# Attention and two mixer blocks on one core: four more pairs of heads take their scores from unsplit fp32 q and k

## Chip, cores and metric

The kernel runs on one core of a Trainium2 chip. The metric is the device time of one execution in microseconds, and lower is better. Three runs of the kernel before took 925.19, 927.50 and 928.23 us; their median, 927.5 us, is the time before.

## What is computed

The reference is a causal attention over 4 batches, 12 heads, 448 positions and a head dimension of 64, followed by two mixer blocks on the joined heads:

```python
scores = scale * np.matmul(q, k.transpose(0, 1, 3, 2))
scores = np.where(mask, -1000000000.0, scores)
scores = scores - np.max(scores, axis=-1, keepdims=True)
attn = np.exp(scores)
attn = attn / (np.sum(attn, axis=-1, keepdims=True) + 1e-09)
attn_out = np.matmul(attn, v)
...
h = np.maximum(xt @ w_tok1, 0.0) @ w_tok2
u = x + h.transpose(0, 2, 1)
h2 = np.maximum(u @ w_ch1, 0.0) @ w_ch2
x = u + h2
...
theta = x @ w_theta
y = w_tok_r @ (x * cos(theta)) + w_tok_i @ (x * sin(theta))
u = x + y
out = u + np.maximum(u @ w_ch, 0.0)
```

All inputs are fp32 or wider (the weights are 64-bit floats), and the kernel keeps close to fp32 accuracy throughout.

## The kernel before

Attention works on pairs of heads: 4 batches of 6 pairs, so 24 pairs, numbered from 0. Pairs 6 to 11 are the second batch. Each pair has seven tiles of scores (the list `TILES`): one of 128 query rows by 128 keys that holds the first 64 positions of both heads, and two each (one per head) with 192, 320 and 448 keys.

There are two ways to make the scores, and the set `NATIVE` (line 30) says which pairs take which. A pair in the set has **native** scores: q and k are loaded into 64 partitions, the other 64 are set to zero by POOL (line 215), and one plain fp32 matmul makes a tile (line 274, `ps_sc<-k_pad,q_raw`). Every other pair has **split** scores: q and k are loaded twice over into 128 partitions, and each is split by ACT and DVE into a high part of the matmul's rounded fp32 type and the rest (`qs`, `kh`, `kl`, lines 231 to 236); two matmuls in that type, with kh and with kl, make a tile (lines 274 and 276), and a tile of 128 or 192 keys is computed with 256 columns. Before, pairs 0 to 7 are native. The lines that matter:

```python
        if b * NPR + pr in NATIVE:
            kr = ap2.tile([P, 2 * S], F32, tag="kh", name="k_pad")
            for t, src in ((kr, k), (qr, q)):
                (nc.vector if b * NPR + pr == 0 else nc.gpsimd).memset(t[64:128], 0.0)
...
            copy_to(pick("qhi"), qs, qr)
            rest_to(pick("qlo"), qs[64:128], qr[64:128], qs[64:128])
            copy_to(pick("khi"), kh, kr)
            rest_to(pick("klo"), kl, kr, kh)
...
        nc.tensor.matmul(ps[:, 0:n], lhsT=lhs, rhs=cut(pp.kh), start=True, stop=pp.kl is None)
        if pp.kl is not None:
            nc.tensor.matmul(ps[:, 0:n], lhsT=lhs, rhs=cut(pp.kl), start=False, stop=True)
```

Buffers: the raw q and k of all pairs share the tag `qk_raw`, which has two buffers. A native pair holds one of them with its q from the load to its last score matmul (its k lies in the tag `kh`, two buffers too). A split pair holds one with q and one with k, and each only until ACT and DVE have split it.

After the scores DVE masks a tile and finds its maximum (line 281, from one of three banks `ps_sc`), ACT takes the exponentials (line 283), and the tile is transposed for the product with v. Pairs 0 to 11 (the set `NATPV`, not changed) have it transposed by PE (line 290) and multiplied in fp32 (line 318). Pairs 12 to 23 have it split into two 16-bit parts `ph` by ACT (line 111) and DVE (line 303), in one of three buffers, transposed by a DMA from SP's queue (`pt<-ph`, line 306) and multiplied in many small matmuls (line 329). Two pairs together give `xg` (line 345, ACT) for a token mixer (lines 354 to 372), whose results fill the four banks `ps_mm` along with everything else on PE; line 367 is the ACT copy that empties one of them.

Beside attention run 72 channel-mixer "units" of 18 matmuls each (`mm3`, lines 170 to 172, 448 columns), placed by the table `UNIT_STEPS`, and the rounding of the 64-bit weights: a raw tile is fetched (line 124, `raw<-in_w_ch_dram`), ACT and DVE round and split it (lines 127 to 138, 118), and it is stored. After attention, from about 530 us, the second mixer runs, which the change does not touch.

The order of the instructions on each engine is set when the program is built: a scheduler with a timeline of its own picks, from what is ready by that timeline, what stands next in each queue, with attention at high priority. Every engine then works through its queue in that order, and a wait at the head holds up all that is behind it. So a change in one place gives other orders from there on.

Of the kernel before, what the change touches and what calls it, by code (L numbers as in the profile page):

```python
# [26 lines left out]
NEG = -1.0e30  # L27
PSC = 32768.0
BUFS = dict(ut=9, h2=6, acc=12, ws=4, wf=2, raw=2, sb=3, ph=3, pt=5)
NATIVE = {0, 1, 2, 3, 4, 5, 6, 7}  # L30
NATPV = {0, 1, 2, 3, 4, 5, 6, 7, 8, 9, 10, 11}
AHEAD, LAG, LOOK = 500, 4, 2
KEEP, UBACK = 6, 16
# [20 lines left out]
def fused(ctx, tc, q, k, v, w_tok1, w_tok2, w_ch1, w_ch2, w_theta, w_tok, w_ch, out):  # L54
# [155 lines left out]
    def prep(b, pr):  # L210
        qr = ap2.tile([P, 2 * S], F32, tag="qk_raw", name="q_raw", bufs=2)
        if b * NPR + pr in NATIVE:
            kr = ap2.tile([P, 2 * S], F32, tag="kh", name="k_pad")
# [12 lines left out]
        nc.sync.dma_start(out=vr, in_=v[b, pr])  # L226
        if b * NPR + pr in NATIVE:
            qs, kh, kl = qr, kr, None
# [558 lines left out]
```

## Time and profile before

| what | value |
|---|---|
| time, median of 3 runs | 927.5 us |
| time of the profiled execution | 925.87 us |
| span of its instructions, first to last | 924.1 us |
| PE busy with matmuls, loading weights | 900.6 us (97%), 825.6 us (89%) |
| DVE, ACT, POOL busy | 633.5 us (69%), 388.2 us (42%), 109.9 us (12%) |
| native scores, first and last start | 4.7 and 108.0 us |
| split scores, first and last start | 113.2 and 462.3 us |
| idle of ACT before line 111's `ph`, for `pt<-ph` | 66.5 us |
| loads of a split pair's q, its k: size, median to landing | 448 KB, 5.3 us; 448 KB, 6.3 us |
| loads of a native pair's k, its q | 224 KB, 3.8 us; 224 KB, 4.1 us |

Times are counted from the span's start. The 1.8 us between the span and the profiled execution's own time lie outside of the first and last instruction. A matmul's time in the trace runs to its modelled end and overlaps the next one's: what a matmul costs PE is the distance from its start to the next start, if nothing waits. PE's share of busy time is therefore not its share of useful time, but idle time before a matmul is real. `PE` rows are matmuls, `PEld` rows their weight loads, `SPq` rows the issues of SP's queue.

### The profile page before, as it was taken

Reading aid. Unit: us, or ns where it says so; the run is one execution under the profiler, and the core shown is the slowest. Engines: PE = TensorE matmul, PEld = TensorE weight load, DVE = VectorE, ACT = ScalarE, POOL = GpSimd, SP = SyncE. Lnnn points to the kernel's source line nnn. Section 1 sums busy time; section 2 is a strip of 40 time slices with the busy share of each in tenths; the row PEclk is TensorE's granted clock in tenths of the full one; section 3 lists DMA queues with packets and bytes.
Section 4 is the critical chain, followed back from the end, with each engine's and each line's share of the span. In section 5 each row is a group of like instructions: output and inputs, shape, how many; then the busy total and the mean of one; then the engine's idle time right before and its main releaser. Section 6 shows DMA issues by size and latency. Waiting matters only on the chain.

```text
span 924.1 us, 15928 instructions
## 1 busy us (share of the span) xinstructions
PE 900.6 (97%) x5820; PEld 825.6 (89%) x5820; DVE 633.5 (69%) x1468; ACT 388.2 (42%) x914; POOL 109.9 (12%) x177
## 2 busy tenths in 40 slices
PE   7999999997999999999999999999999999999998
PEld 5988999896898898989899999999999999999997
DVE  6799797998987777467774288845864566575341
ACT  6788677675655555344532144321211212202100
POOL 2110000000000000000000000021631233242120
PEclk9999999998999999999999999999999999999999
DMA  6677994789999979699797899864505225054033
GB/s 184 190 254 254 360 335 172 251 300 272 260 316 317 285 207 263 223 275 290 199 322 244 280 326 369 281 195 132 184 1 162 78 86 179 19 162 128 6 133 129
DMA packets 104687, 199.17 MB, mean 216 GB/s; under 512 B 60896, under 2 KB 72992, under 8 KB 104608
## 3 DMA queue, kind: packets, MB, share of 16 engines
q1 hardware_dynamic: 103296, 196.35, 67.9%
q0 software_dynamic: 1152, 1.57, 0.9%
q8 instruction: 46, 0.75, 0.3%
q14 instruction: 33, 0.27, 0.1%
q10 hardware_dynamic: 160, 0.23, 0.1%
HBM read 149.36 MB, written 34.60 MB: 199 GB/s over the span
## 4 chain that ended last, share of the span: by engine, by line
PE 81%; DMA 10%; DVE 6%; issue 1%; ACT 1%; SPq 1%; ACTq 0%; DVEq 0%
PE ps_mm L170 18%; PE ps_mm L172 18%; PE ps_mm L171 18%; DMA pt<-ph 6%; PE ps_sc L274 3%; PE ps_sc L172 3%; PE ps_sc L170 3%; PE ps_sc L171 3%; PE ps_pv L318 3%; PE ps_pv L329 3%; DMA raw<-in_w_ch_dram 2%; PE ps_mm L290 2%; PE ps_sc L276 1%; PE ps_mm L355 1%; PE ps_mm L356 1%
## 5 line engine op out<-in xcount | busy, mean ns | idle before, releaser
L170 PE MATMUL ps_mm<-h,ws 128*128 128x448 f32 x432 | 159.4, 370 | 2.1 <-DMA ws<-w_c 1.3
L171 PE MATMUL ps_mm<-h,ws 128*128 128x448 f32 x432 | 159.2, 369 | 0.0
L172 PE MATMUL ps_mm<-h,ws 128*128 128x448 f32 x432 | 158.6, 368 | 0.0
L172 PE MATMUL ps_mm<-ut,ws 128*128 128x448 f32 x288 | 106.4, 369 | 0.0
L170 PE MATMUL ps_mm<-ut,ws 128*128 128x448 f32 x288 | 106.3, 369 | 0.0
L171 PE MATMUL ps_mm<-ut,ws 128*128 128x448 f32 x288 | 105.9, 368 | 0.0
L283 ACT ACTIVATE sb<-sb,mx 128x192 f32<-128x192 f32 (+3 forms) x168 | 89.3, 532 | 32.4 <-DVE mx L281 31.4
L170 PEld LDWEIGHTS ps_mm<-h,ws 128*128 128x128 f32 x432 | 81.2, 188 | 9.7 <-DMA ws<-w_c 1.6
L172 PEld LDWEIGHTS ps_mm<-h,ws 128*128 128x128 f32 x432 | 81.2, 188 | 7.0
L171 PEld LDWEIGHTS ps_mm<-h,ws 128*128 128x128 f32 x432 | 81.2, 188 | 6.8
L281 DVE CUSTOM_DVE_ANT_0 sb<-ps_sc,mask 128x192 f32<-128x192 f32 (+3 forms) x168 | 74.2, 455 | 10.2 <-PE ps_mm L290 5.8
L114 POOL TENSOR_SCALAR ut<-acc 128x448 fp32r<-128x448 f32 x24 | 17.4, 731 | 474.9 <-PE ps_mm L171 454.3
L591 ACT ACTIVATE tmp<-ps_sc 128x384 f32<-128x384 f32 x28 | 13.5, 482 | 132.3 <-PE ps_sc L172 132.1
L303 DVE SCALAR_TENSOR_TENSOR ph<-sb,ph 128x64 f16<-128x64 f32 (+3 forms) x156 | 42.8, 318 | 33.2 <-ACT ph L111 32.4
L318 PE MATMUL ps_pv<-v_raw,ptf 128*128 128x128 f32 (+1 forms) x456 | 63.6, 275 | 1.4 <-issue 0.9
L318 PEld LDWEIGHTS ps_pv<-v_raw,ptf 128*128 128x128 f32 x456 | 59.6, 192 | 5.7 <-issue 2.3
L111 ACT ACTIVATE ph<-sb 128x192 f16<-128x192 f32 (+3 forms) x84 | 36.5, 443 | 66.9 <-DMA pt<-ph 66.5
L172 PEld LDWEIGHTS ps_mm<-ut,ws 128*128 128x128 f32 x288 | 54.2, 188 | 4.5 <-issue 0.2
L170 PEld LDWEIGHTS ps_mm<-ut,ws 128*128 128x128 f32 x288 | 54.2, 188 | 4.5 <-issue 0.2
L171 PEld LDWEIGHTS ps_mm<-ut,ws 128*128 128x128 f32 x288 | 54.2, 188 | 4.2
L388 DVE SCALAR_TENSOR_TENSOR h<-ps_mm,h 128x448 fp32r<-128x448 f32 x48 | 29.7, 619 | 31.3 <-ACT h L387 31.2
L598 ACT ACTIVATE tmp<-tmp 128x384 f32<-128x384 f32 x28 | 14.7, 526 | 86.0 <-DVE tmp L596 86.0
(152 smaller groups left out, 2113.7 us busy)
## 6 DMA issues: line engine op xcount, KB each, us to landing
ws<-w_c SPq DMA_DIRECT2D x107, 768.0 KB, 5.5
raw<-in_w_ch_dram SPq DMA_DIRECT2D x30, 768.0 KB, 6.3
w_c<-ws SPq DMA_DIRECT2D x30, 768.0 KB, 6.6
q_raw<-in_q_dram SPq DMA_DIRECT2D x16, 448.0 KB, 5.3
k_raw<-in_k_dram SPq DMA_DIRECT2D x16, 448.0 KB, 6.3
v_raw<-in_v_dram SPq DMA_DIRECT2D x24, 288.0 KB, 4.9
x2d<-acc SPq DMA_DIRECT2D x24, 224.0 KB, 4.8
acc<-x2d SPq DMA_DIRECT2D x24, 224.0 KB, 3.6
```

Of the source, the lines that this page charges most:

```text
L111: nc.scalar.activation(dst, src, AF.Copy, scale=scale)
L170: nc.tensor.matmul(ps, lhsT=ka(a[:, 0]), rhs=kb(b[:, 0]), start=first, stop=False)
L171: nc.tensor.matmul(ps, lhsT=ka(a[:, 0]), rhs=kb(b[:, 1]), start=False, stop=False)
L172: return nc.tensor.matmul(ps, lhsT=ka(a[:, 1]), rhs=kb(b[:, 0]), start=False, stop=last)
L274: nc.tensor.matmul(ps[:, 0:n], lhsT=lhs, rhs=cut(pp.kh), start=True, stop=pp.kl is None)
L281: pp.first = nc.vector.tensor_tensor_reduce(out=dst, in0=src, in1=msk, op0=ALU.add, op1=ALU.min, scale=-0.125, scalar=3.0e38, accum_out=pp ...
L283: pp.last = nc.scalar.activation(sb[:, 0:kk], sb[:, 0:kk], AF.Exp, bias=pp.mx[:, j:j + 1], scale=-1.0, accum_out=pp.sm[:, j:j + 1])
L290: nc.tensor.transpose(pst[:, u * P:(u + 1) * P], full[:, c0 + u * P:c0 + (u + 1) * P], ident)
L303: nc.vector.scalar_tensor_tensor(out=dst, in0=sb[:, c0:c1], scalar=PSC, in1=hi[:, c0:c1], op0=ALU.mult, op1=ALU.subtract)
L318: pp.pv = nc.tensor.matmul(pp.ps[:, reg:reg + n], lhsT=pt[:, u], rhs=pp.v[0][:, vt * D:vt * D + n], start=(u == 0), stop=(u == len(blks) - 1))
L329: pp.pv = nc.tensor.matmul(pp.ps[:, reg:reg + D], lhsT=pt[:, blk], rhs=pp.v[c][:, vt * D:(vt + 1) * D], start=(n == 0), stop=(n == len(job ...
L388: gates[0] = nc.vector.scalar_tensor_tensor(out=t[:, 1], in0=ps[:, 0:S], scalar=0.0, in1=f32v(t[:, 0]), op0=ALU.max, op1=ALU.subtract)
```

## The change

Pairs 8 to 11 join the set. Nothing else in the source differs:

```diff
-NATIVE = {0, 1, 2, 3, 4, 5, 6, 7}
+NATIVE = {0, 1, 2, 3, 4, 5, 6, 7, 8, 9, 10, 11}
```

By instructions: PE has 28 split score matmuls at line 274 and 28 at line 276 fewer for 28 native ones more (8 tiles of 448, 8 of 320, 8 of 192 and 4 of 128 keys). ACT has 8 copies of 128x896 fewer, DVE 4 of `kl` and 4 of `qs` fewer, POOL 8 memsets of 64x896 more. SP's queue has 8 loads of 128x896 fewer for 8 of 64x896 more.

The built orders differ in many places from pair 8 on. Three of them follow. The first is **SP's queue** from the loads of pair 11 or 12 to those of pair 14. The `L222` and `L224` rows are loads of a split pair's q and k. Before, pairs 12, 13 and 14 are `q_raw_2189`, `q_raw_2378` and `q_raw_2670`:

```order
L222 DMA q_raw_2189<-in_q_dram 128x896
L124 DMA raw_1811<-in_w_ch2_dram 128x1536
L224 DMA k_raw_2191<-in_k_dram 128x896
L448 DMA w_c2_0_2_107<-ws_1807 128x1536
L124 DMA raw_1895<-in_w_ch2_dram 128x1536
L226 DMA v_raw_1916<-in_v_dram 128x576
L124 DMA raw_1966<-in_w_ch2_dram 128x1536
L448 DMA w_c2_0_3_108<-ws_1891 128x1536
L448 DMA w_c2_1_4_115<-ws_1962 128x1536
L222 DMA q_raw_2378<-in_q_dram 128x896
L224 DMA k_raw_2380<-in_k_dram 128x896
```

and in the change pairs 12 and 13 are `q_raw_2147` and `q_raw_2330`:

```order
L448 DMA w_c2_1_4_115<-ws_1926 128x1536
L222 DMA q_raw_2147<-in_q_dram 128x896
L124 DMA raw_1954<-in_w_ch1_dram 128x1536
L448 DMA w_c2_0_4_109<-ws_1950 128x1536
L224 DMA k_raw_2149<-in_k_dram 128x896
L124 DMA raw_2098<-in_w_ch1_dram 128x1536
L448 DMA w_c2_0_5_110<-ws_2094 128x1536
L222 DMA q_raw_2330<-in_q_dram 128x896
L224 DMA k_raw_2332<-in_k_dram 128x896
```

Before, q of pair 12 stood ahead of the stores `w_c2_0_2` to `w_c2_1_4`; in the change it stands behind them. In the built program of the change pair 11's q lies in one buffer of `qk_raw`, and q of 12, k of 12, q of 13 and k of 13 all have the address of the other, which q of pair 10 held before them. Before, the q and k of pair 12 have two addresses, and so have those of 13.

The second place is **ACT** in the change, while pair 11 (`sb`, `sm_2136`) begins. `kh_2156` is pair 12's, `qs_2336` pair 13's; `ps_mm_2016` to `ps_mm_2061` are banks that the token mixer fills:

```order
L357 ACTIVATE h1_2015<-ps_mm_2016 128x256
L111 ACTIVATE kh_2156<-k_raw_2149 128x896
L357 ACTIVATE h1_2015<-ps_mm_2031 128x256
L367 ACTIVATE acc_2051<-ps_mm_2046 128x448
L111 ACTIVATE qs_2336<-q_raw_2330 128x896
L367 ACTIVATE acc_2066<-ps_mm_2061 128x448
```

The copy that empties `ps_mm_2061` stands behind the split of pair 13's q. The next unit on PE, `ps_mm_2115`, has that bank's address.

The third place is **PE** where pair 12's product with v begins. Before, between the last matmul of the first three tiles and the first of the next tile (`pt_2469`):

```order
L329 MATMUL ps_pv_2495<-v_mid_2202,pt_2444 128x64
L274 MATMUL ps_sc_2723<-kh_2387,qs_2384 128x256
L276 MATMUL ps_sc_2723<-kl_2389,qs_2384 128x256
L354 MATMUL ps_mm_2502<-xg0_2282,wt1_146 128x256
L354 MATMUL ps_mm_2517<-xg0_2282,wt1_146 128x256
L363 MATMUL ps_mm_2532<-ident2_128,x0_154 128x64
L365 MATMUL ps_mm_2532<-ident_123,x0_154 128x128 x3
L274 MATMUL ps_sc_2757<-kh_2387,qs_2384 128x256
L276 MATMUL ps_sc_2757<-kl_2389,qs_2384 128x256
L329 LDWEIGHTS pt_2469
```

and in the change the same place begins as follows:

```order
L329 MATMUL ps_pv_2447<-v_mid_2160,pt_2396 128x64
L354 MATMUL ps_mm_2454<-xg0_2237,wt1_146 128x256
L354 MATMUL ps_mm_2469<-xg0_2237,wt1_146 128x256
L363 MATMUL ps_mm_2484<-ident2_128,x0_154 128x64
L365 MATMUL ps_mm_2484<-ident_123,x0_154 128x128 x3
L355 MATMUL ps_mm_2454<-xg1_2238,wt1_146 128x256
L356 MATMUL ps_mm_2454<-xg0_2237,wt1_146 128x256
L354 MATMUL ps_mm_2454<-xg0_2237,wt1_146 128x256
```

There the whole token mixer (24 matmuls of 256 columns), 8 transposes by PE, 6 score matmuls and 6 matmuls of the mixer's second half stand ahead of the next tile's first line-329 matmul.

## Rows read from the trace of the kernel before

**Rows 1.** Windows: us; PE, PEld, DVE, ACT, POOL busy (x count); PEclk, DMA share, GB/s

```profile
150.00:175.00 25.00, 25.00 (x171) 23.80 (x170) 22.41 (x48) 17.79 (x40) 0.00 (x0) 1.00 0.70 242
175.00:200.00 25.00, 23.96 (x160) 21.87 (x159) 23.32 (x50) 16.55 (x38) 0.00 (x0) 1.00 0.74 258
200.00:225.00 25.00, 18.76 (x139) 17.12 (x138) 21.02 (x58) 16.38 (x40) 0.00 (x0) 0.86 1.07 290
225.00:250.00 25.00, 22.91 (x198) 20.55 (x196) 23.02 (x58) 15.22 (x38) 0.00 (x0) 1.00 1.00 267
```

**Rows 2.** Waits from 175 to 250 us: us in total, times, longest

```profile
PE ps_pv L329 <- DMA pt<-ph: 5.7, 3, 3.0
...
PE ps_mm L170 <- ACT acc L367: 0.8, 1, 0.8
```

**Rows 3.** Timeline of PE, 211 to 220 us: start, us, instruction [idle before <-releaser]

```profile
211.42 0.20 PE L329 MATMUL ps_pv<-v_raw,pt 128*128 128x64 bf16 x1 [0.62 <-DMA pt<-ph]
...
215.27 0.50 PE L354 MATMUL ps_mm<-xg,wt 128*128 128x256 f32 x2 [2.60 <-ACT xg L111]
...
219.72 0.23 PE L329 MATMUL ps_pv<-v_raw,pt 128*128 128x64 bf16 x1 [3.02 <-DMA pt<-ph]
```

**Rows 4.** Windows, the stretch behind those waits

```profile
220.00:224.00 4.00, 4.00 (x30) 4.00 (x28) 3.31 (x12) 2.72 (x7) 0.00 (x0) 0.55 1.04 359
```

**Rows 5.** Timeline of PE: native scores, each with the instruction behind it

```profile
28.52 0.70 PE L274 MATMUL ps_sc<-k_pad,q_raw 128*128 128x320 f32 x2
29.06 0.49 PE L290 MATMUL ps_mm<-ident,sb 128*128 128x128 f32 x3
29.38 0.92 PE L274 MATMUL ps_sc<-k_pad,q_raw 128*128 128x448 f32 x2
30.14 0.50 PE L318 MATMUL ps_pv<-v_raw,ptf 128*128 128x128 f32 x3
...
78.67 0.49 PE L274 MATMUL ps_sc<-k_pad,q_raw 128*128 128x192 f32 x2
79.00 0.60 PE L290 MATMUL ps_mm<-ident,sb 128*128 128x128 f32 x4
```

**Rows 6.** Timeline of PE: split scores, first matmul and the instruction behind the second

```profile
169.22 0.28 PE L274 MATMUL ps_sc<-kh,qs 128*128 128x256 f32 x1
...
169.46 0.36 PE L170 MATMUL ps_mm<-h,ws 128*128 128x448 f32 x1
...
202.41 0.32 PE L274 MATMUL ps_sc<-kh,qs 128*128 128x320 f32 x1
...
202.71 0.31 PE L274 MATMUL ps_sc<-kh,qs 128*128 128x320 f32 x1
...
207.74 0.37 PE L274 MATMUL ps_sc<-kh,qs 128*128 128x448 f32 x1
...
208.15 0.36 PE L171 MATMUL ps_mm<-ut,ws 128*128 128x448 f32 x1
```

**Rows 7.** Tile q_raw: count, ns min/median/max, first to last start; its loads' landing

```profile
L111 ACT ACTIVATE qs<-q_raw x16: 934/937/952, 96.1 to 416.6; 128x896 fp32r<-128x896 f32 x16
L118 DVE TENSOR_TENSOR qs<-q_raw,qs x16: 1087/1089/1091, 97.1 to 418.0; 64x896 fp32r<-64x896 f32 x16
...
DMA to landing us min/median/max: 2.1/4.6/10.5
```

**Rows 8.** Tile k_raw, the same columns

```profile
L111 ACT ACTIVATE kh<-k_raw x16: 934/940/958, 104.8 to 415.6; 128x896 fp32r<-128x896 f32 x16
L118 DVE TENSOR_TENSOR kl<-k_raw,kh x16: 1071/1086/1093, 106.5 to 416.6; 128x896 fp32r<-128x896 f32 x16
...
DMA to landing us min/median/max: 4.2/6.3/7.5
```

**Rows 9.** Timeline: pair 12's first tile, its score on PE and its maximum on DVE

```profile
194.62 0.37 PE L274 MATMUL ps_sc<-kh,qs 128*128 128x256 f32 x1
...
199.60 0.28 DVE L281 CUSTOM_DVE_ANT_0 sb<-ps_sc,mask 128x128 f32<-128x128 f32 x1
```

## The prediction, made before the change was run

> **What bounds the kernel now.** I read the windows first. Pairs 8 to 11 were scored between 113 and 198 us. From 150 to 175 us PE is busy for all of its 25.00 us, and no wait of PE shows there; DVE is busy for 22.41 us of them [rows 1]. So in this stretch the program moves as fast as PE's queue, and DVE, though close, is not what ends last. From 175 us that changes: PE loses 25.00 - 23.96 = 1.0 us, then 6.2, then 2.1 us, 9.4 in all [rows 1]. The list of waits says for what: 5.7 us for three landings of DMA transposes of pairs 12 and 13, the first pairs that are transposed so, and 0.8 for ACT emptying a bank [rows 2]. The timeline puts most of it in one place, the start of pair 12's product with v: 0.62 us before its first matmul, 2.60 before the token mixer, which waits for ACT's xg, and 3.02 before the next tile's product [rows 3]. After these pauses the granted clock reads 0.55 from 220 to 224 us, with PE busy throughout [rows 4]: some 90% of that stretch at the lower of its two levels, 1.2 of 2.4 GHz, which costs about half of 3.6 us, 1.8 us. A reader should see two things: work added to PE before 175 us costs its full time, and between 200 and 224 us lie 6.2 us of waits and 1.8 us of slow clock that a different order could win back.
>
> **PE's own work.** What a tile costs is the distance between starts [rows 5, 6]. 448 keys: native 30.14 - 29.38 = 0.76 us, split 208.15 - 207.74 = 0.41, so +0.35. 320 keys: 29.06 - 28.52 = 0.54 against 202.71 - 202.41 = 0.30, +0.24. 192 keys: 79.00 - 78.67 = 0.33 against 169.46 - 169.22 = 0.24 (the split form computes 256 columns), +0.09. 128 keys: two thirds of 0.33 is 0.22, an estimate, against 0.24, -0.02. A pair has two of each of the first three and one of the last: 2 x 0.68 - 0.02 = 1.34. Four pairs: **+5.4 us**. No gap of PE hides it: it falls before and beside 113 to 198 us, where the waits are 1.0 us in all.
>
> The Trainium skill has a rule that speaks against the change: by "FP8 and Floating Point Precision", TensorE Precision Notes, true fp32 takes four passes through the array. With a split matmul as one pass (0.205, 0.15 and 0.12 us here), four passes would make 0.82, 0.60, 0.35 and 0.23 us, a pair +1.63 and the term +6.5 us; the rows give a little less than four passes, and the sum goes by the rows.
>
> **What ACT, DVE and POOL lose and gain.** A split costs ACT 0.937 + 0.940 us and DVE 1.089 + 1.086 us [rows 7, 8]; four pairs make 7.5 us on ACT and 8.7 us on DVE. Where PE is full this is worth nothing by itself: DVE only comes closer to being on time. The 8 memsets fall on POOL, which does nothing at all from 150 to 250 us [rows 1], and a pair's loads have the time of a whole pair, some 20 us. I count both as nothing; without that cover a late memset would hold SP's queue, and through it the weight loads. The smaller loads (64 partitions for 128) I count as nothing too: no PE wait before 175 us is one for a load.
>
> **The hand-over from pair 11 to pair 12.** Here the change makes a chain. q of 12, k of 12, q of 13 and k of 13 go through one buffer, each after the split of the one before, and the first only after pair 10's last score matmul, because pair 11's native q holds the other buffer. Counted from there: q of 12 lands after 4.6 (the median), ACT and DVE split it in 0.94 + 1.09 [rows 7], 6.6 us; k of 12 takes 6.3 + 0.94 + 1.09 [rows 8], 14.9 us; q of 13 takes 4.6 + 0.94 on ACT, 20.4 us. Behind that copy stands ACT's line 367, about half a microsecond (I take 0.5), which empties the bank that the next unit needs: 20.9 us. Between the same score and that unit PE's queue holds 50 matmuls of 448 columns at 0.205 (half of the 0.41 above, 10.2 us), 24 of the token mixer at 0.12 (2.9), four native tiles of 128, 192, 192 and 320 keys (1.4), and 37 small fp32 matmuls and transposes, some of them twice as long (about 5.4 in all): 19.9 us. So at median landings PE waits **1.0 us**, about what it loses there already [rows 1]: net 0. That is the most uncertain term. If everything lands at the least (2.1, 4.2, 2.1) it is 0 and the present 1.0 us is gone; one q that takes 10.5 us adds 5.9. DVE stands still during these landings, so pair 12 begins with DVE late, and it is late already: the first tile's score stands at 194.62 and DVE takes it up at 199.60, 5.0 us later [rows 9]. PE's cover between that score and the first line-329 matmul grows by only 1.2 us (17.2 for 16.0). I take **+0.7 us** more at the first wait, between 0 and +3.
>
> **Pair 12's product.** In the profile the next tile's product starts 219.72 - 211.42 = 8.3 us after the first [rows 3]; that is the way through ACT, DVE and one more transpose, because there are only three buffers `ph`. PE had 1.8 us of work in it, 0.6 for the first three tiles and 1.2 behind them. In the new order the whole token mixer and more stands there: 24 x 0.12 + 8 transposes at 0.11 + 6 score matmuls (0.84) + 6 x 0.205 = 5.9 us, with the first tiles 6.5. Of the waits 8.3 - 6.5 = 1.8 us remains for 2.60 + 3.02 = 5.6: **-3.8 us**. With pauses so much shorter I count half of the slow clock as gone, **-0.9**. Bounds: 0 if ACT and DVE are later by as much, -7.4 if both go fully. The native pairs show some short waits of their own in the first 100 us; I put **+0.6** on pairs 8 to 11, between 0 and 2.
>
> Sum: 5.4 + 0.0 + 0.7 - 3.8 - 0.9 + 0.6 = **+2.0 us**. The profiled execution took 925.87 us, with a span of 924.1, so the changed one should take about 927.9. It lies 1.6 below the median of the three runs; on 927.5 the forecast is **929.5 us**.
>
> **The rivals.** First, slower: the landings decide. PE's work covers 19.9 us of a chain of 20.9, so from there on each microsecond of a late landing is one of the end time. For it: q's landing reaches 10.5 us [rows 7], and in the new order weight tiles stand between these loads on the same queue. Against it: the DMA share from 150 to 200 us is 0.70 to 0.74, not the 1.07 of later [rows 1]. With one load at its maximum 929.5 + 5.9 = 935.4 us.
>
> Second, faster: DVE is what makes the waits, and 8.7 us less of it let pair 12 start on time, so that all waits of 175 to 224 us go. For it: the 5.0 us by which DVE is late at pair 12 [rows 9]. Against it: the splits of 12 and 13 stay, and the splits that go are those before. Then 5.4 - (1.0 + 0.6 + 5.6 + 1.8) = -3.6: 923.9 us.
>
> Third, no change: the forecast holds, and the remaining transposes' wait at pair 13, 5.7 - 0.62 - 3.02 = 2.1 us [rows 2, 3], goes as well, since pair 12 is spread over more work: 927.4 us.
>
> That the change does not do what it says can be left out: the counts of instructions show 28 native matmuls for 56.
>
> **How the numbers follow.** A measurement here can tell 0.3% from no change, 2.8 us: 924.7 to 930.3. The forecast, about 928 to 932, has a chance of 0.45, of which 0.31 lie within 0.3% and 0.14 above. The late landings, 932 to 938, have 0.26, all above. The faster case has 0.16, of which 0.01 lies within. The third has 0.13, all within. So faster 0.15, within 0.3% 0.45, slower 0.40. The forecast's own range is 928 to 932. For 8 in 10 the range takes in the faster case's point and the late landings up to one load at its maximum with a microsecond and a half on top: 923.8 to 937.
>
> **What would show it.** Right: 28 more native score matmuls at 0.76, 0.54 and 0.33 us from start to start; PE without idle time up to about pair 11; a wait of some 1 us for ACT line 367 there; less than 3 us of PE's waits for xg and `pt<-ph` at pair 12, and a granted clock of 1 behind it. Wrong: a wait of several microseconds for ACT or DVE behind a q or k load before pair 12 (the first rival), no waits from 175 to 224 us (the second), or waits at pair 12 as long as before.

## The result and the profile after

The changed kernel took 933.59 us (median of 6 runs, 932.36 to 937.58), the kernel before beside it 926.40 (6 runs). The ratio is 1.0091, 95% interval 1.0072 to 1.0111: slower by 0.9%. Measured once more, beside another set of runs of before, it was 1.0058 (1.0035 to 1.0080), so the change costs some 5 to 8 us where 2 were forecast. The profiled execution of the change took 933.34 us, its span is 931.6: 7.5 us more than the span of before.

The page's part 1, first line (busy us, share, instructions), of the change:

```profile
PE 906.6 (97%) x5820; PEld 826.7 (89%) x5820; DVE 627.0 (67%) x1460; ACT 381.7 (41%) x906; POOL 115.9 (12%) x185
```

PE is busy for 6.0 us longer (900.6 before) and idle for 1.5 us longer (25.0 for 23.5). DVE and ACT were each busy for 6.5 us less (the splits that went make 8.6 and 7.5 us, instruction by instruction), and the kernel is slower all the same. The windows of the change, with the columns of [rows 1]:

```profile
150.00:175.00 25.00, 25.00 (x156) 22.23 (x156) 22.33 (x49) 15.21 (x36) 1.64 (x2) 1.00 0.80 260
175.00:200.00 25.00, 23.11 (x146) 20.96 (x144) 19.56 (x43) 14.80 (x34) 0.00 (x0) 1.00 0.61 207
200.00:225.00 25.00, 22.11 (x166) 20.52 (x165) 24.23 (x62) 17.89 (x40) 0.00 (x0) 1.00 0.93 285
225.00:250.00 25.00, 22.23 (x168) 19.32 (x167) 18.89 (x49) 15.64 (x40) 0.00 (x0) 1.00 1.02 268
...
250.00:475.00 225.00, 221.98 (x1856) 201.88 (x1855) 161.86 (x441) 113.33 (x279) 0.00 (x0) 0.99 0.94 264
475.00:931.60 456.60, 450.05 (x2407) 416.90 (x2403) 264.44 (x522) 100.01 (x211) 94.47 (x150) 1.00 0.52 169
```

From 175 to 250 us PE is idle for 1.89 + 2.89 + 2.77 = 7.6 us where it was 9.4 [rows 1], and in this execution the clock no longer falls there. Behind 250 us it is the other way round. For the kernel before the two last windows read:

```profile
250.00:475.00 225.00, 222.78 (x1833) 202.34 (x1832) 161.63 (x440) 114.37 (x281) 0.00 (x0) 1.00 0.95 267
475.00:924.10 449.10, 444.64 (x2374) 412.56 (x2372) 257.50 (x505) 96.19 (x202) 94.89 (x150) 1.00 0.51 167
```

Idle there is 3.0 + 6.6 = 9.6 us for 2.2 + 4.5 = 6.7, and the granted clock of the change falls once more, just behind two waits at 318 and 320 us:

```profile
320.00:324.00 4.00, 4.00 (x20) 3.73 (x18) 2.70 (x12) 2.93 (x11) 0.00 (x0) 0.59 1.12 245
```

In that window the kernel before reads 1.00. The 4.00 us at 0.59 cost 1.6 us. The places, from the timeline of the change (PE and ACT):

```profile
182.26 0.95 ACT L111 ACTIVATE kh<-k_raw 128x896 fp32r<-128x896 f32 x1 [0.25 <-issue]
...
188.85 0.95 ACT L111 ACTIVATE qs<-q_raw 128x896 fp32r<-128x896 f32 x1 [4.93 <-DMA q_raw<-in_q_dram]
189.70 0.53 ACT L367 ACTIVATE acc<-ps_mm 128x448 f32<-128x448 f32 x1
...
190.28 0.47 PE L170 MATMUL ps_mm<-h,ws 128*128 128x448 f32 x1 [1.89 <-ACT acc L367]
...
217.79 0.20 PE L329 MATMUL ps_pv<-v_raw,pt 128*128 128x64 bf16 x1
...
219.42 0.50 PE L354 MATMUL ps_mm<-xg,wt 128*128 128x256 f32 x2 [0.81 <-ACT xg L111]
...
222.50 0.39 PE L355 MATMUL ps_mm<-xg,wt 128*128 128x256 f32 x1 [2.08 <-DVE xg L118]
...
229.19 0.20 PE L329 MATMUL ps_pv<-v_raw,pt 128*128 128x64 bf16 x1 [1.26 <-DMA pt<-ph]
...
318.22 0.20 PE L329 MATMUL ps_pv<-v_raw,pt 128*128 128x64 bf16 x1 [0.60 <-DMA pt<-ph]
...
319.64 0.20 PE L329 MATMUL ps_pv<-v_raw,pt 128*128 128x64 bf16 x1 [1.01 <-DMA pt<-ph]
...
483.99 0.44 PE L170 MATMUL ps_mm<-h,ws 128*128 128x448 f32 x1 [2.17 <-DMA ws<-w_c]
```

The first four rows are the hand-over as the prediction described it: ACT waits 4.9 us for pair 13's q, line 367 stands behind its split, and PE waits 1.89 us for that. The load itself was not slow: SP's queue issued it at 184.36 us, behind the split of pair 12's k, and it landed in 4.5 us, about the median [rows 7]. Pair 12's product with v starts at 217.79 us. Its waits are shorter than before, and the longest is for DVE's xg (line 118), where the prediction had named ACT's. The last three rows have no counterpart of their size in the kernel before; its longest wait behind 250 us is 1.3 us, also for a load of weights (`ws<-w_c`).

The native tiles cost what was said. Timeline of PE, pair 8:

```profile
119.20 0.70 PE L274 MATMUL ps_sc<-k_pad,q_raw 128*128 128x320 f32 x2
119.74 1.95 PE L318 MATMUL ps_pv<-v_raw,ptf 128*128 128x128 f32 x16
121.52 0.92 PE L274 MATMUL ps_sc<-k_pad,q_raw 128*128 128x448 f32 x2
121.93 0.71 PE L172 MATMUL ps_mm<-ut,ws 128*128 128x448 f32 x1
122.48 0.36 PE L170 MATMUL ps_mm<-ut,ws 128*128 128x448 f32 x1
```

320 keys take 0.54 us. Of 448 keys the trace shows 0.41 where a unit's matmul follows, and the rest in that matmul, which lasts 0.71 for 0.36; together 122.48 - 121.52 = 0.96, less 0.205 for the unit's own, 0.755.

### The profile page after: what moved, and what is told of

Read it like the earlier page. It is cut to its first block, busy times and chain, and to the rows that moved or that the text cites. A ratio compares the mean times of both kernels' runs of the same rounds, so it can differ in the third digit from the quotient of the medians.

```text
span 931.6 us, 15927 instructions
## 1 busy us (share of the span) xinstructions
PE 906.6 (97%) x5820; PEld 826.7 (89%) x5820; DVE 627.0 (67%) x1460; ACT 381.7 (41%) x906; POOL 115.9 (12%) x185
## 3 DMA queue, kind: packets, MB, share of 16 engines
q0 software_dynamic: 1152, 1.57, 0.8%
## 4 chain that ended last, share of the span: by engine, by line
PE 74%; DMA 13%; DVE 8%; ACT 2%; issue 2%; DVEq 0%; ACTq 0%; SPq 0%
PE ps_mm L170 17%; PE ps_mm L172 17%; PE ps_mm L171 17%; DMA pt<-ph 8%; PE ps_sc L274 3%; PE ps_sc L172 3%; PE ps_sc L170 3%; PE ps_sc L171 3%; PE ps_pv L318 2%; PE ps_pv L329 2%; DVE sb L281 1%; DMA w_c<-ws 1%; PE ps_mm L290 1%; DVE wf L137 1%; PE ps_mm L613 1%
## 5 line engine op out<-in xcount | busy, mean ns | idle before, releaser
L274 PE MATMUL ps_sc<-k_pad,q_raw 128*128 128x192 f32 (+3 forms) x168 | 55.3, 429 | 5.9 <-DMA k_pad<-in_k_dram 4.9
L170 PE MATMUL ps_sc<-th,ut 128*128 128x384 f32 x144 | 50.1, 348 | 0.0
```

Source lines behind the costliest of these rows:

```text
L170: nc.tensor.matmul(ps, lhsT=ka(a[:, 0]), rhs=kb(b[:, 0]), start=first, stop=False)
```

## The experiments

Theory: PE's own 5.4 us come on top up to pair 11, and the waits behind are moved by the order that the scheduler (the planner, below) builds. The rivals were the loads through one buffer (1), PE's work vanishing in waits (2), the order alone (3), the relief of DVE being worth its time (4, 5), landings that differ in each execution (6), and one tile's path through ACT, DVE and the transpose (7). Ratios are to the kernel before, run in turn with it on the same chip. PE's idle time (span less busy, us) by stretch tells where a profiled execution differs; each number is from that run's windows. The last column is its mean granted clock: 0.001 of it is about 0.9 us at full speed (0.001 x 930).

| run | ratio | to 175 us | 175 to 250 | 250 to 475 | behind | clock |
|---|---|---|---|---|---|---|
| before | 1 | 7.5 | 9.4 | 2.2 | 4.5 | 0.996 |
| change | 1.0091 | 7.9 | 7.6 | 3.0 | 6.6 | 0.998 |
| change again | 1.0058 | 8.0 | 5.2 | 3.0 | 6.6 | 0.994 |
| third matmul | 1.0074 | 7.6 | 1.4 | 8.5 | 5.0 | 0.998 |
| q of its own | 1.0046 | 13.9 | 3.3 | 3.5 | 5.1 | 0.998 |
| the same, before | 1.0045 | 12.2 | 8.4 | 3.8 | 5.0 | 0.995 |
| dummy split | 1.0112 | 8.9 | 7.3 | 3.0 | 4.8 | 0.992 |
| gated, change | 1.0028 | 7.8 | 3.1 | 4.3 | 4.5 | 0.994 |
| gated, before | 1.0046 | 8.9 | 7.8 | 5.5 | 4.2 | 0.993 |
| ten native | 1.0051 | 9.6 | 8.6 | 3.4 | 5.7 | 0.995 |
| four native, gated | 1.0034 | 11.4 | 7.9 | 3.0 | 4.4 | 0.991 |
| six native | 1.0066 | 10.8 | 7.1 | 4.4 | 5.4 | 0.994 |
| four `ph`, before | 1.0032 | 7.9 | 7.7 | 5.8 | 5.9 | 0.996 |
| four `ph`, change | 1.0152 | 7.8 | 8.0 | 6.3 | 6.9 | 0.992 |

**PE's work alone.** Edit on the kernel before:

```diff
+        if 8 <= pp.b * NPR + pp.pr < 12:
+            nc.tensor.matmul(ps[:, 0:n], lhsT=lhs, rhs=cut(pp.kl), start=True, stop=True)
         nc.tensor.matmul(ps[:, 0:n], lhsT=lhs, rhs=cut(pp.kh), start=True, stop=pp.kl is None)
```

> The kernel before, with one more split matmul (kl against q) ahead of each score tile of pairs 8 to 11; it is overwritten by the next one, so the result is the same and only PE has more work. Loads, splits and buffers stay as before. By the distances of the trace, 0.205, 0.15 and 0.12 us, a pair has 2 x 0.475 + 0.12 = 1.07 us more, four pairs 4.3 us. Theory (the change is slower because PE is the bound up to pair 11 and has more to do there; the rest is the waits behind it in another order): about 926.4 + 4.3 = 930.7 us, and up to 2 more or less by the order behind pair 11. Rival 1 (the one buffer for the loads of pairs 12 and 13 makes the loss): nothing of the 2 us beyond PE's work, and no wait for line 367 before pair 12; 929 to 931. Rival 2 (PE's new work fills the waits of 200 to 224 us, and the loss comes from elsewhere): 926 to 928.

Measured 933.04 us, 1.0074 (1.0046 to 1.0102), some 4 to 9 us slower for 4.3 of PE's work, above the time that rival 2 gave. Its waits from 175 to 250 us and then from 250 to 500 us (the list of waits: us in total, times, longest):

```profile
PE ps_pv L331 <- DMA pt<-ph: 1.1, 2, 0.9
PE ps_mm L356 <- ACT xg L111: 0.2, 1, 0.2
...
PE ps_pv L331 <- DMA pt<-ph: 5.7, 5, 1.9
PE ps_pv L331 <- DVE v_mid L118: 1.5, 1, 1.5
```

Pair 12's waits are nearly gone, without any relief of ACT or DVE and with all loads as before; and as in the change, waits stand behind 250 us that were not there. So half of rival 2 shows in the trace: PE's new work fills the waits up to 250 us (1.4 us idle for 9.4), and what is lost stands behind them (8.5 + 5.0 us idle for 2.2 + 4.5). The run does not show that added work comes out at the end as it is.

**The loads' buffer.** Edit on the change, and the same on the kernel before:

```diff
-        qr = ap2.tile([P, 2 * S], F32, tag="qk_raw", name="q_raw", bufs=2)
+        if b * NPR + pr in NATIVE:
+            qr = ap2.tile([P, 2 * S], F32, tag="qs", name="q_raw")
+        else:
+            qr = ap2.tile([P, 2 * S], F32, tag="qk_raw", name="q_raw", bufs=2)
```

> The changed kernel, with the q of native pairs in the tag qs (two buffers, which native pairs do not use) and no longer in qk_raw, so that the loads of pairs 12 and 13 have both buffers of qk_raw to themselves and need not wait for pair 10's last score. Theory (PE's work, plus moved waits): the wait of 1.9 us for line 367 goes, and at best the 2.1 us for DVE's xg too: 929.6 to 931.7 against 933.6. Rival 1 (the loads through one buffer are what makes it slower beyond the forecast): all that is over PE's own work goes, 926 to 929.5. Rival 3 (the 5.6 us that were lost behind 250 us come from the order of the queues there, which any edit shuffles): the part up to 250 us gets shorter by about 2 us and the part behind it moves by several us either way.

> The same edit (q of native pairs in the tag qs) on the kernel before, where pairs 0 to 7 are native. No wait of PE there was one for these loads, so theory and rival 1 both say about 926.4, within 1.5 us. Rival 3 (order alone shifts the time by several us) says that it may move by 2 to 5 us although nothing that PE waited for is touched; the place must then lie behind 250 us.

Measured 931.55 us, 1.0046 (1.0032 to 1.0060), and 932.57 us, 1.0045 (1.0024 to 1.0066). The wait for line 367 is gone in the first, and the stretch from 175 to 250 us has 3.3 us of idle time for 7.6. But the second became slower too, though in the kernel before PE waited for nothing that the edit touches. The timelines of PE show one reason, at the start, in the first (change with q of its own) and in the second:

```profile
10.43 0.55 PE L277 MATMUL ps_sc<-k_pad,q_raw 128*128 128x128 f32 x1 [10.43 <-DMA k_pad<-in_k_dram]
...
8.33 3.12 PE L277 MATMUL ps_sc<-k_pad,q_raw 128*128 128x128 f32 x8 [8.33 <-DMA k_pad<-in_k_dram]
```

The first score of the change starts at 4.89 us. So the first time lies in the theory's range only with some 5.5 us in it that the theory did not have. With the buffers free from the start, the planner put q and k of the first split pair at the head of SP's queue, ahead of pair 0's own k. So the edit was repeated with those loads tied to the pair before:

```diff
-            loads[b * NPR + pr] = nc.sync.dma_start(out=qr, in_=q[b, pr])
...
-            nc.sync.dma_start(out=kr, in_=k[b, pr])
+            with tc.issue_after(loads[b * NPR + pr - 1].ins):
+                loads[b * NPR + pr] = nc.sync.dma_start(out=qr, in_=q[b, pr])
+                nc.sync.dma_start(out=kr, in_=k[b, pr])
```

> The changed kernel with q of native pairs in the tag qs, and with the loads of a split pair's q and k issued only after the load of the pair before it. Without that the planner had put q and k of pair 12 ahead of pair 0's in SP's queue (their buffer was free from the start), and the first score began at 10.4 us in place of 4.9. The loads of pairs 12 and 13 have two buffers again. Theory (PE's work is the base, the waits come on top, each in its own place): the run with q of its own was at a ratio of 1.0046, of which the 5.5 us at the start go: 0.9985 to 1.001 of before, some 925 to 928, although PE has 5.4 us more to do than before. Rival 3 (each build has an order of its own, and the waits behind 200 us move by several us whatever is done): 922 to 933, with a start as before and waits behind 250 us that differ from those of the run with q of its own.

> The same two edits on the kernel before (pairs 0 to 7 native). PE has the work of before, and nothing that PE waited for in before is changed. Theory: before's time, within 1.5 us. Rival 3: 3 us or more away from before, with the difference in waits behind 170 us.

Measured 930.45 us, 1.0028 (1.0012 to 1.0045), and 931.46 us, 1.0046 (1.0024 to 1.0068). The start is as before in both. With twelve native pairs the waits from 175 to 250 us are these two:

```profile
PE ps_mm L358 <- ACT xg L111: 1.6, 1, 1.6
PE ps_pv L333 <- DMA pt<-ph: 1.5, 1, 1.5
```

and with eight (line 371 is line 367 of the other kernels):

```profile
PE ps_pv L333 <- DMA pt<-ph: 4.1, 3, 3.4
PE ps_mm L358 <- ACT xg L111: 2.0, 1, 2.0
PE ps_mm L170 <- ACT acc L371: 0.7, 1, 0.7
```

The theory's numbers were missed twice: the first is 2 us above its range, the second too, with 7.8 + 5.5 us idle in the two middle stretches. That is rival 3's forecast. Between these two, four native pairs more cost nothing: 930.45 for 931.46. So the hand-over's wait is real and can be taken out, but without it the kernel is still 3 us slower than before; and two edits without a cost that the theory could name moved the kernel before by some 4 us each (in the first of them the late start is part of it).

**The relief of ACT and DVE.** Edit on the change, for pairs 8 to 11:

```diff
+            if b * NPR + pr >= 8:
+                qd = ap2.tile([P, 2 * S], F32R, tag="qs", name="qd")
+                copy_to("A", qd, qr)
+                rest_to("D", qd[64:128], qr[64:128], qd[64:128])
+                kd = ap2.tile([P, 2 * S], F32R, tag="qs", name="kd")
+                copy_to("A", kd, kr)
+                kl2 = ap2.tile([P, 2 * S], F32R, tag="kl", name="kd2")
+                rest_to("D", kl2, kr, kd)
```

> The changed kernel, in which ACT and DVE still make the split of q and k of pairs 8 to 11 (two copies, two subtractions each) into tiles that nobody reads, so the result is the same; PE has the native matmuls. It gives back to ACT and DVE the 7.5 and 8.7 us that the change took from them. Theory (their relief is worth nothing where PE is full): 933.6, within 2 us. Rival 4 (the relief is worth part of its time, because DVE is what is late at pair 12): 936 to 942, with longer waits for DVE and for xg at 200 to 230 us.

Measured 937.56 us, 1.0112 (1.0084 to 1.0141). That is 2 us over the change's first ratio, with overlapping intervals, and 5 over its second, without. Its list of waits has a line for xg and one for DVE, the engines that rival 4 named:

```profile
PE ps_mm L362 <- ACT xg L111: 3.1, 1, 3.1
...
PE ps_mm L170 <- DVE wf L134: 2.1, 1, 2.1
```

But they do not bear rival 4 out. Its place was 200 to 230 us: there PE waits 3.1 us for xg, where it waited 2.9 and 2.3 in the two traces of the change, and not for DVE. The wait for DVE stands at 281 us and is one for the rounding of weights (line 134). In all PE is idle for 24.0 us, for 25.0 and 22.7 in the change. What differs most is the clock. From 225 to 250 us the dummy split has 0.82, where the first trace of the change has 1.00 and the second 0.93:

```profile
225.00:250.00 25.00, 22.45 (x165) 20.25 (x166) 23.68 (x60) 17.11 (x41) 0.00 (x0) 0.82 0.96 301
```

In all six executions of this run the mean granted clock is 0.990 to 0.992, in the twelve of the change 0.992 to 0.998; on average that is 0.0036 lower, about 3 us of 932. Why is not shown. This run, too, has an order of its own, and 2 to 5 us is about what edits without a direct cost moved. So it leaves open what the relief is worth.

**Other numbers of native pairs.** The set alone was edited, to pairs 0 to 9 and to pairs 0 to 5; the run with pairs 0 to 3 also has the two gated edits.

> Half of the change: pairs 8 and 9 join the set, 10 and 11 stay split; no other edit. PE has 2 x 1.34 = 2.7 us more. Theory, if the rest of the loss goes with PE's work: half of the change's 7.5, 3 to 4.5 us over before. Rival 1 (the loads of the first split pairs behind a native pair): the first split pair is now 10, whose loads stand in a stage without waits, so only PE's 2.7 us or less. Rival 3: anything from -2 to +8, by the order.

> Pairs 0 to 3 alone are native, with the two edits of the gated run (q of native pairs in qs, loads of split pairs behind those of the pair before). PE has 4 x 1.34 = 5.4 us less than before, ACT 7.5 and DVE 8.7 us more, between 35 and 113 us, where DVE is busy for 90 percent. Theory (PE is the bound also there): 5.4 less than the same with eight native pairs, about 921 to 923. Rival 5 (in that stretch DVE's lateness is what ends last, and splits cost their DVE time): 926 to 932, with waits of PE for DVE before 113 us.

> The other direction: pairs 0 to 5 alone are native, pairs 6 and 7 take split scores too; no other edit. PE has 2 x 1.34 = 2.7 us less than before; ACT has 3.8 and DVE 4.4 us more, between about 75 and 113 us, where DVE was busy for 90 percent of the time before. Theory (PE's work comes off the time where PE is the bound, the rest is order): 2.7 us less than before, 925 to 926 beside a before of about 928, and 2 more or less by the order; if so it beats both kernels. Rival 5 (DVE ends last up to 113 us, as in the run with four native pairs): 928 to 932, with more waits of PE before 113 us.

Measured: ten native pairs 932.98 us, 1.0051 (1.0024 to 1.0078); four 930.78 us, 1.0034 (1.0017 to 1.0050); six 932.51 us, 1.0066 (1.0036 to 1.0095). None beats the kernel before. With ten pairs the hand-over comes two pairs earlier, and PE waits 1.1 us for line 367 at 145 us, soon after a q for which ACT waited 1.5 us: the same kind of wait at its new place, where rival 1 expected none. The 4.7 us that the run lost (2.2 to 7.2) fit the theory and rival 3. With four, PE's 5.4 us less of work did not show: the time is that of the gated kernel before, as rival 5 had it, with 11.4 us idle up to 175 us for 8.9. With six the windows show one reason why less native work doesn't help. From 75 to 100 us, first the kernel before:

```profile
75.00:100.00 25.00, 23.92 (x166) 21.38 (x165) 21.68 (x54) 17.56 (x46) 2.04 (x2) 1.00 0.81 290
```

and with pairs 6 and 7 split:

```profile
75.00:100.00 25.00, 21.58 (x160) 19.14 (x159) 24.60 (x59) 21.33 (x53) 0.00 (x0) 1.00 0.84 302
```

DVE is busy for 24.60 of 25.00 us and ACT for 21.33, PE is idle for 3.4 where it was 1.1. The list of waits from 20 to 113 us with pairs 6 and 7 split names both engines:

```profile
PE ps_sc L274 <- DVE mx L281: 1.9, 3, 0.7
PE ps_mm L170 <- ACT acc L367: 1.3, 2, 0.6
```

Before, the first is 0.5 us there and the second does not show. So in that stretch PE waits for DVE and ACT, and the native form takes work from the right engines; at pairs 8 to 11 [rows 1] PE was full. Up to 175 us idle time grew by 3.4 us, which uses up the 2.7 that PE has less to do; the rest of the loss is not explained by this.

**Four buffers for ph.** `ph=4` for `ph=3` in `BUFS`, on the kernel before and on the change:

> The kernel before, with four buffers for ph in place of three; no other edit. The prediction put pair 12's waits down to these three buffers. Theory: of the waits before, 2.6 us for ACT's xg, 3.0 and 2.1 us for transposes, most go, and the slow clock behind them: 4 to 8 us less, 919 to 924 beside a before of 927.6. Rival 3 (order decides, not the buffers): the waits at 210 to 250 us stay above 6 us in all, time 924 to 932. Rival 7 (the path through ACT, DVE and the transpose of one tile is what lasts): the first waits shrink by less than 2 us in all.

> The changed kernel, with four buffers for ph in place of three. Theory: its waits for xg (0.8 and 2.1 us) and for transposes at 229, 318, 320 and 423 us (3.8 in all) shrink by half or more, the 1.9 us for line 367 and PE's 5.4 us stay: 3 to 5 us less than the change, +2 to +5 over before. If the change's PE work is what counts once pair 12's waits are gone, it is then about 5 us slower than the kernel before with four buffers. Rival 3: the difference of the two is anything from -3 to +9.

Measured 930.43 us, 1.0032 (1.0016 to 1.0049), and 940.68 us, 1.0152 (1.0122 to 1.0183). In the first the wait for xg is gone, and the waits for transposes take its place (list of waits, 175 to 250 us):

```profile
PE ps_pv L329 <- DMA pt<-ph: 6.7, 4, 3.9
PE ps_mm L170 <- ACT acc L367: 0.8, 1, 0.8
```

6.7 us, where xg and transposes had 8.3 before: the first waits shrank by 1.6, as rival 7 had it; the time and the waits also fit rival 3. In the timeline of PE the buffer shows all the same: the fourth tile's product starts at 215.01 us, 3.8 us after the first (8.3 before [rows 3]), and now the fifth waits longest, 3.90 us, until 221.14. In the second, line 367 costs 2.9 us, behind a q for which ACT waited 6.1 us, and 6.7 us of waits for transposes stand behind 250 us. Both expectations of the theory failed, and the difference of the two, 10 to 11 us, is also above rival 3's.

**The change once more.**

> The change itself once more, with a trace of another execution. Theory (its order makes its waits): ratio between 1.007 and 1.011, and the waits at the same places as in the first trace: about 1.9 us for line 367, 2 to 3 for xg and its rest, 1 to 2 for transposes near 229 and near 318 us, 2 near 484, each within 1 us. Rival 6 (the waits behind 250 us are landings that fall otherwise in each execution): other places or sizes behind 250 us, the sum there between 3 and 12 us.

Measured 932.76 us, a ratio of 1.0058, below the expected 1.007 to 1.011. Timeline of PE in this execution:

```profile
190.50 0.47 PE L170 MATMUL ps_mm<-h,ws 128*128 128x448 f32 x1 [1.75 <-ACT acc L367]
...
220.89 0.51 PE L354 MATMUL ps_mm<-xg,wt 128*128 128x256 f32 x2 [0.77 <-ACT xg L111]
...
223.67 0.58 PE L355 MATMUL ps_mm<-xg,wt 128*128 128x256 f32 x1 [1.57 <-DVE xg L118]
...
318.73 0.20 PE L329 MATMUL ps_pv<-v_raw,pt 128*128 128x64 bf16 x1 [0.61 <-DMA pt<-ph]
...
320.14 0.20 PE L329 MATMUL ps_pv<-v_raw,pt 128*128 128x64 bf16 x1 [1.00 <-DMA pt<-ph]
...
484.56 0.44 PE L170 MATMUL ps_mm<-h,ws 128*128 128x448 f32 x1 [2.00 <-DMA ws<-w_c]
```

These waits stand at the same places as in the first trace, within 0.6 us each, those behind 250 us within 0.2. So in two executions of one built program the long waits behind 250 us are the same, and rival 6 falls. Between 200 and 250 us some do differ: the wait near 229 us (1.26 in the first trace) is missing, against the expectation, the one near 241 us is 0.21 for 1.40, and 0.76 us at 218.94 are new.

## Why the prediction was right in sign and short in size

The time lies in the wide range, 923.8 to 937 us, and on the side to which the forecast pointed, but above the forecast's own range of 928 to 932: some +5 to +8 us, not +2. That the wide range held it is partly luck: its upper end was there for a load that lands late, and no such load decided. By its steps:

- **PE's own work, +5.4: held as work.** The tiles measured 0.755 and 0.54 us, PE had no idle time from 113 to 175 us, and its busy time grew by 6.0, a slow clock in both traces included. The Trainium skill ("FP8 and Floating Point Precision", TensorE Precision Notes) counts four passes for true fp32; the trace shows 0.755 / 0.205 = 3.7 split matmuls' time, so the rows were the better price.
- **Short waits at the native pairs, +0.6: not seen.** From 113 to 175 us PE is not idle at all; the 0.4 us more up to 175 us (7.9 for 7.5) lie before 113 us. Memsets and smaller loads at nothing: held there. That no wait of PE before 175 us is one for a load was read wrongly: the longest, 4.7 us before the first score, is one for pair 0's k.
- **Hand-over, a wait of 1.0 for a net of 0: mechanism right, size 1.9 and 1.75.** The run with q of its own took it away, the run with ten native pairs moved it.
- **Pair 12, +0.7 - 3.8 - 0.9 = -4.0: about right in sum, for a reason that is only half right.** The first wait was to be 1.3 us, 0.62 [rows 3] and 0.7; it was nothing in the first execution and 0.76 in the second. From 175 to 250 us idle time fell by 1.8 and the slow clock's 1.8 [rows 4] went: -3.6, the hand-over included. In the second execution idle time fell by 4.2 and some of the clock was lost. The waits for xg and transposes were 4.2 and about 3 us, where less than 3 was said. The wrong piece is the 8.3 us, taken as a fixed way through ACT, DVE and one more transpose: in the change the next tile's product starts 229.19 - 217.79 = 11.4 us after the first, still with 1.26 us of waiting, so the way itself became longer. That three buffers `ph` set it is right only for that one tile: a fourth buffer let it start 3.8 us after the first, but moved the long wait to the fifth tile and took only 1.6 us off the waits in all. That more PE work ahead of and inside the stretch shortens its waits fits the third matmul (1.4 us idle), in which the order differs as well.
- **The failed step, which makes most of the miss, is one that the sum did not have: the waits behind 250 us.** "Half of the slow clock as gone" and waits "won back" were taken as lasting. But idle time behind 250 us grew by 2.9 us and the slow clock at 320 us took 1.6, 4.5 in all. With it the sum is 5.4 + 0.4 - 3.6 + 4.5 = 6.7 of the 7.5 us between the two profiled executions; 0.8 stay open. The prediction told the reader that a change in one place gives other orders from there on, and still priced the later orders at nothing.
- **Relief of ACT and DVE at nothing: open.** The dummy split was 2 to 5 us slower than the change, which is about the spread between orders here, and its waits for DVE do not make that.

Of the rivals, late landings did not decide (pair 13's q took 4.5 us), and the waits of 175 to 224 us did not all go; pair 13's 2.1 us for transposes went, as the third rival had it, but decided nothing.

What is shown: what the tiles add to PE's work, the hand-over, and that the longer waits behind 250 us are the same in two executions of one built program. How much of the added work comes out at the end is not shown: in the third matmul, and between the two gated runs, waits shrank where PE had more to do. What is only argued: that the planner's order, and not something else in the change, makes those later waits. Every edit of the set builds another order, so order and edit could not be parted here. The same four pairs cost 5 to 8 us as they stand, nothing with the gated loads, and 10 to 11 with four `ph`; PE's 5.4 lies within that, and a spread of several us around it is probably what a new order is worth in this kernel. All seven edits of the kernel before that were run came out 3 to 7 us slower by their ratios; why its order has so little idle time from 250 to 475 us (2.2, for 3.0 or more in each run of the table) stays open.

## What to carry to other kernels

Moving work from one engine to another can be expected to pay only in the stage where the first is what ends last: here four native pairs more were bought with PE's time where PE had no idle time, while two fewer put DVE at 98% and PE at waits for DVE and ACT. Where a planner builds the order, price the change by its own work and put several microseconds of uncertainty on everything behind it, on the side of loss if the present order is a good one; an edit without a direct cost shows how large that spread is. A wait that is shortened counts as a gain only when the trace shows that no later stage takes it back.

## What was not expected of the hardware

In one program a slow clock and a wait seem to have stood for each other. In the second execution of the change PE ran from 223.67 us on at a lower clock:

```profile
224.00:228.00 4.00, 4.00 (x20) 4.00 (x20) 3.71 (x12) 2.42 (x7) 0.00 (x0) 0.50 1.00 395
```

0.50 is the lower of its two levels, 1.2 of 2.4 GHz, and it came behind waits of 0.76, 0.77 and 1.57 us; in the first execution the waits there were 0.81 and 2.08 us and the clock stayed at 1.00. There PE then waited 1.26 and 1.40 us at 229 and 241 us, in the second 0.21 us at 241 alone. Both executions come to the same span (931.6 and 931.9 us) with mean clocks of 0.998 and 0.994 and 25.0 and 22.7 us of idle time: part of what the clock took is probably time that PE would have waited for other engines. Two executions are all that speaks for it, and the dummy split had a lower clock than the second of them (0.992) with more idle time (24.0 us), not less.
